# Five reciprocals of softmax sums as a power with exponent minus one on GpSimd, in a two-stage attention kernel with a token mixer

## The chip, the cores and the metric

The kernel runs on one core of a Trainium2 chip. The metric is the device time of one execution in microseconds (us). The kernel before takes 119.73 us, the median of three runs (119.31 to 119.91). The core has five engines that run at the same time, each through its own queue of instructions, in order: TensorE (PE in the profile; its weight loads are PEld), VectorE (DVE), ScalarE (ACT), GpSimd (POOL) and SyncE (SP). They wait for one another by semaphores. Loads are issued by GpSimd, stores by SyncE.

## The reference

For each of 8 batches and 8 heads there are 576 queries, keys and values of 64 numbers and 32 "packed" queries p. The first attention lets p attend to the keys; the second lets the queries attend to the result, so its softmax is only 32 wide. A token mixer with three weight matrices follows.

```python
def sm_attn(qq, kk, vv):
    s = scale * np.matmul(qq, kk.transpose(0, 1, 3, 2))
    s = s - np.max(s, axis=-1, keepdims=True)
    a = np.exp(s)
    a = a / (np.sum(a, axis=-1, keepdims=True) + 1e-09)
    return np.matmul(a, vv)
p_packed = sm_attn(p, k, v)
x = sm_attn(q, p_packed, p_packed)        # heads put side by side: [8, 576, 512]

wq, wk = x @ w_q, x @ w_k                 # 64 wide
W_tok = scale2 * einsum('bsd,btd->bst', wq, wk)
out = np.maximum(einsum('bst,btd->bsd', W_tok, x), 0.0) @ w_out
```

The change touches the division in the second attention: the sums are inverted, and the exponentials are multiplied with the inverses.

## The kernel before

All work goes batch by batch, b = 0 to 7, as a list of small operations, each a Python function named in `ops`. The string SCHEDULE (lines 10 to 59) is the program: it lists every operation once, in the order in which it is issued, for example `sm0@3g`: operation sm0 of batch 3 on GpSimd ("v" is VectorE, "s" ScalarE; a digit behind a colon is a bank of PSUM). Since every engine works its queue in order, the list sets the order on each engine, and batches overlap as the list interleaves them. Nothing is rearranged afterwards; only the waits between engines are derived from the tiles that the operations read and write. SLOTS gives the number of buffers of each tile, reused in turn.

The second softmax of a batch works on a tile of 128 partitions x 36 units x 32 scores (36 units hold the 8 heads and 9 blocks of 64 queries):

- e0, e1, e2 (L470, L482): scores on TensorE, into PSUM.
- mx0, mx1, mx2 (L498) and sb0, sb1, sb2 (L502): the maxima and the subtraction on VectorE.
- x0 (L531): the exponential on ScalarE, over 128x1152.
- sm0: the sums over 32. On VectorE one reduction (L537, batches 0, 2 and 7); on GpSimd a tree of five additions that halves the width (L540, three times L542, L543; batches 1, 3, 4, 5 and 6).
- rr0 (L547): the reciprocal of the 128x36 sums, on VectorE for all eight batches.
- ml0, ml1, ml2 (L551): exponentials times reciprocals, for the units 0 to 15, 16 to 31 and 32 to 35, into the bf16 tile a2. Each of the 24 runs on the engine that the list names; five run on VectorE (ml2@0, ml1@2, ml0@3, ml1@4, ml2@6), the other 19 on GpSimd.
- at0 (from ml0's units) and at1 (from ml1's and ml2's) (L571, L574): transposes of a2 on TensorE, evicted by ae0 and ae1. Later matmuls (g, L675 and L683) read a2 itself.

Other operations that stand near: LQ, LK and LV issue the loads of a batch's q, k and v on GpSimd (L148); rc1 (L369) is the reciprocal of the first softmax's sums, 128x2, and rm (L408) uses it on GpSimd; pp (L430) and pte evict the packed values of the first attention; wkx (L650) prepares an operand of g; w1 (L203) is a matmul on zeros that keeps TensorE warm and whose result nobody reads.

Where the five reciprocals stand in the list, with what is next to them on GpSimd's queue:

```
... sm0@1g rc1@3 rr0@1 LQ@4 ... ml1@1g ... ml2@1g ... ml0@1g
... sm0@3g ... LV@7 y@2 rr0@3 ml1@3g ml2@3g rc1@5 ... ml0@3v
... sm0@4g ... rr0@4 ... ml2@4g ml1@4v ... rm@6 ml0@4g
... sm0@5g rr0@5 ... ml2@5g ... ml0@5g ... ml1@5g
... sm0@6g rr0@6 ml2@6v ... ml1@6g ... ml0@6g
```

Of the kernel before, what the change touches and what calls it, by code (L numbers as in the profile page):

```python
# [20 lines left out]
    e2@1:1 mx2@1 kt1@3:2 w1@0f:4 LQ@3 ae0@0s ae1@0s LK@5 sb1@1 ke1@3s wk@0f:4 sb0@1 sb2@1 wz@0  # L21
    wke@0s kt0@3:5 ke0@3v LK@6 xt0@2f:6 wq@0:7 xe0@2v s0@3:0 rc1@2 rm@2 wkx@0 x0@1 nm0@3 wqe@0s
    qt1@2:5 qe1@2v xt1@2f:4 xe1@2s g@0f:3 ge@0s qt0@2:7 ex0@3 y@0:3 pv@2:5 qe0@2v pp@2 ye@0s m0@0:73
    r00@0v ex1@3 r01@0s pt@2c:5 pte@2v m1@0:01 xt1@3c:2 e0@2c:5 r11@0s e2@2:7 sm0@1g rc1@3 rr0@1
    LQ@4 xe1@3v ml1@1g mx2@2 ml2@1g r10@0s mx0@2 kt0@4:6 ke0@4v sb2@2 sb0@2 pq@2:3 ml0@1g pq@1:0
    pqe@2s pqe@1s LV@4 kt1@4:1 ke1@4s e1@2f:4 mx1@2 LQ@5 at1@1f:7 ae1@1s w1@0f:5 xt0@3c:6 xe0@3s
    s0@4:0 at0@1c:5 sb1@2 o2@0c:7 ae0@1v rm@3 wk@1f:5 nm0@4 wq@1:6 LK@7 LQ@6 wz@1 pv@3:3 wkx@1 x0@2
# [3 lines left out]
    e0@3f:0 r10@1s LV@6 ae0@2s mx0@3 e1@3f:7 mx1@3 LQ@7 rm@4 kt0@5:4 r00@1s wk@2f:6 ke0@5s sb0@3  # L31
    m2@1f:5 r2@1s o3@0f:1 oe3@0s sb1@3 wz@2 e2@3:0 kt1@5:3 mx2@3 wke@2s wq@2:7 sb2@3 kt1@6:0 x0@3
    sm0@3g wqe@2s ke1@5v kt0@6:2 s0@5:3 wkx@2 o1@0f:6 ke1@6v g@2f:7 ge@2s nm0@5 ex1@5 oe1@0v qt1@4:0
    ex0@5 qt0@4:7 qe0@4s ke0@6v o2@1f:6 qe1@4v xt1@5f:3 pv@4:0 LV@7 y@2:4 rr0@3 ml1@3g ml2@3g rc1@5
    oe2@1s xt0@5f:7 ye@2s ml0@3v at0@3f:2 pp@4 pt@4c:0 xe1@5s m1@2:45 r11@2s xe0@5v m0@2:61 r00@2s
    r10@2s r01@2s pte@4v e2@4:3 ae0@3v mx2@4 e1@4f:0 o4@1f:2 sb2@4 rm@5 mx1@4 st1@0 e0@4f:7 sb1@4
    mx0@4 oe4@1s at1@3f:6 ae1@3s o0@1f:5 oe0@1s s0@6:0 pq@4:4 pqe@4s sb0@4 x0@4 qt0@5:3 nm0@6
    qt1@5:6 ex0@6 qe1@5v o1@1c:4 oe1@1v kt0@7:5 kt1@7:6 wk@3f:4 ex1@6 rc1@6 sm0@4g ke0@7s xt1@6f:0
    qe0@5s ke1@7v xe1@6v wz@3 wke@3v wq@3:1 wqe@3s wkx@3 s0@7:5 qt0@6:0 qe0@6s qt1@6:2 nm0@7 ex0@7
    ex1@7 qe1@6v xt0@6f:4 o3@2f:1 rr0@4 g@3f:0 ge@3s o2@2f:2 oe2@2s st0@1 pv@5:5 ml2@4g ml1@4v  # L40
    xe0@6v y@3:3 ye@3s xt0@7f:7 xe0@7s at1@4f:2 pp@5 pt@5f:5 pte@5v oe3@2s xt1@7f:4 rm@6 ml0@4g
    at0@4f:0 m2@3f:6 r2@3s rc1@7 ae1@4v e0@5f:5 xe1@7s mx0@5 rm@7 ae0@4s e1@5f:3 o3@1f:1 oe3@1s
    o4@3f:7 wk@4f:2 oe4@3s e2@5:1 mx1@5 sb0@5 pq@5:0 pqe@5s sb1@5 wz@4 wke@4s pv@6:5 m0@3:07 mx2@5
    sb2@5 x0@5 m1@3:13 r10@3s wq@4:4 pp@6 r01@3s pt@6c:5 r00@3v r11@3s wqe@4s st2@3 qt0@7:6 pte@6v
    wkx@4 o0@2c:0 qe0@7v st0@0 e1@6c:7 mx1@6 g@4c:1 ge@4s e2@6:3 mx2@6 sb2@6 qt1@7:5 e0@6c:4 sb1@6
    o1@3c:1 mx0@6 pv@7:2 st1@1 st1@2 sm0@5g rr0@5 qe1@7s y@4:6 oe1@3s sb0@6 o1@2f:5 ye@4s st2@1
    m1@4:71 m0@4:46 pp@7 pq@6:3 oe1@2v pt@7c:2 oe0@2s st0@2 x0@6 ml2@5g o2@3c:0 r10@4s r01@4v ml0@5g
    at0@5c:6 pte@7v e0@7c:2 pqe@6v r11@4s ae0@5v e2@7:3 mx2@7 e1@7c:7 ml1@5g pq@7:1 at1@5c:5 r00@4s
    mx0@7 mx1@7 o0@3c:4 pqe@7s sb2@7 o3@3c:6 ae1@5s wk@5c:1 sb1@7 sb0@7 sm0@6g rr0@6 ml2@6v oe0@3s
    wq@5:5 oe3@3s wz@5 wke@5s o2@4c:7 wkx@5 oe2@3v st1@3 x0@7 sm0@7v ml1@6g o0@4c:3 rr0@7 ml0@6g  # L50
    wqe@5s ml0@7g ml2@7g oe0@4s g@5c:1 ge@5s o3@4c:0 oe2@4s at0@6c:6 oe3@4s y@5:4 ye@5s ae0@6v st0@3
    at1@6c:1 ae1@6v o1@4c:3 m2@5c:7 m0@5:40 r00@5v m1@5:15 oe1@4v st0@4 at0@7c:2 r2@5s r01@5s r11@5s
# [10 lines left out]
    wk=3, wkx=3, wqT=3, g=2, y=3, r=2, reluX=2, o_sb0=2, o_sb1=2, ox=2,  # L63
# [5 lines left out]
def kernel(  # L69
# [12 lines left out]
    nc = tc.nc  # L82
    fp32 = mybir.dt.float32
# [14 lines left out]
    P = 128  # L98
    NJ = S // 64
    NU = 36  # L100
# [6 lines left out]
    sbp = ctx.enter_context(tc.tile_pool(name="sbp", bufs=1))  # L107
# [7 lines left out]
    S_ = [{} for _ in range(B)]  # L115
# [5 lines left out]
    def tile(name, shape, dtype, b, key=None):  # L121
        key = key or name
        if key not in S_[b]:
            S_[b][key] = sbp.tile(shape, dtype, tag=f"{name}{(b // 2 if name in PAIRED else b) % SLOTS[name]}", name=name)
        return S_[b][key]
# [56 lines left out]
    nc.vector.memset(zero, 0.0)  # L182
    pT_bd = sbp.tile([P, B, 4, 2, L], bf16, name="pT_bd")
    nc.vector.memset(pT_bd, 0.0)
    mask = sbp.tile([P, 2, Dh], fp32, name="mask")
    nc.vector.memset(mask, 0.0)
    for g in range(4):
# [355 lines left out]
        nc.gpsimd.tensor_tensor(rs, t[:, :, 0:1], t[:, :, 1:2], op=ADD)  # L543

    @op
    def rr0(b):
        nc.vector.reciprocal(tile("rr", [P, NU, 1], fp32, b), S_[b]["rs"])  # L547

    def ml(i, b, on):
        r = slice(16 * i, min(16 * i + 16, NU))  # L550
# [245 lines left out]
    for item in SCHEDULE.split():  # L796
        name, rest = item.split("@")
# [35 lines left out]
```

## Time and profile before

| | |
|---|---|
| median of three runs | 119.73 us |
| the profiled execution, its time | 119.49 us |
| its span (first to last instruction) | 117.7 us |
| mean granted TensorE clock | 0.993 |
| busy, TensorE | 105.6 us |
| busy, VectorE | 91.1 us |
| busy, ScalarE | 88.0 us |
| busy, GpSimd | 60.1 us |
| HBM traffic over the span | 337 GB/s |

The times in the rows of the profile are in us from the span's start; "L551" is line 551 of the kernel. A timeline row gives the start, the duration, the engine, the line, the operation, what it writes and reads with the shapes, the number of instructions merged, and in brackets how long the engine sat idle before it and what released it. A group's row gives the busy time, the mean in nanoseconds and the idle time before its instructions. The chain of waits is followed back from the last instruction to what released each step. The ends of matmuls are modelled, and times on GpSimd are rough.

### The profile page before, as it was taken

To read this page: it belongs to the slowest core of one execution; us is meant where nothing else is said; L and a number is where in the kernel's file an instruction comes from. 1 tells how busy PE (TensorE), PEld (TensorE's weight loads), DVE (VectorE), ACT (ScalarE), POOL (GpSimd) and SP (SyncE) were. 2 spreads that over 40 slices of the span, in tenths; PEclk is the share of its full clock that TensorE was granted. 3 is DMA by queue.
4 is the path that set the end of the run, shared out by engine and by line. 5 is a ranking of instruction groups with operands and counts; after the bars stand their busy time and mean duration, and the time that the engine had idled before them with its cause. 6 is when DMAs were issued, how large, how long until landed. Compare 5 with 4: busy or idle time off the path is not lost.

```text
span 117.7 us, 4778 instructions
## 1 busy us (share of the span) xinstructions
PE 105.6 (90%) x2065; PEld 68.6 (58%) x2081; DVE 91.1 (77%) x184; ACT 88.0 (75%) x164; POOL 60.1 (51%) x88
## 2 busy tenths in 40 slices
PE   5997587887988999999999999999999999999950
PEld 1234456575855857778665875867566566545520
DVE  5326958999989989999999999698999967571420
ACT  5005574699879899899589999999898967678430
POOL 6965342278558994645981283606697780000000
PEclk9999999999999999999999999999999999999997
DMA  3999999999999999999999999999932174464793
GB/s 41 291 269 198 213 202 207 208 198 208 208 208 206 207 207 209 209 207 208 251 249 207 207 207 282 220 205 362 354 138 89 57 305 166 199 267 184 288 369 145
DMA packets 17925, 25.47 MB, mean 216 GB/s; under 512 B 2160, under 2 KB 14448, under 8 KB 17904
## 3 DMA queue, kind: packets, MB, share of 16 engines
q0 software_dynamic: 13920, 14.49, 73.2%
q1 hardware_dynamic: 3984, 10.68, 24.0%
q8 instruction: 16, 0.26, 0.8%
q14 instruction: 5, 0.04, 0.1%
HBM read 30.21 MB, written 9.44 MB: 337 GB/s over the span
## 4 chain that ended last, share of the span: by engine, by line
PE 63%; DMA 23%; DVE 7%; issue 2%; POOL 2%; ACT 1%; DVEq 0%; POOLq 0%
PE psum L755 27%; DMA k_sb<-in_k_dram 16%; PE psum L304 8%; DMA q_sb<-in_q_dram 7%; PE psum L421 3%; PE psum L714 3%; PE psum L571 3%; PE psum L660 3%; PE psum L376 3%; PE psum L628 2%; PE psum L470 2%; PE psum L345 2%; PE psum L683 1%; DVE nmax L355 1%; DVE kT L141 1%
## 5 line engine op out<-in xcount | busy, mean ns | idle before, releaser
L755 PE MATMUL psum<-w_out,r 128*64 128x512 bf16 (+1 forms) x208 | 30.9, 380 | 0.6 <-issue 0.3
L551 POOL TENSOR_TENSOR a<-e,rr 128x512 bf16<-128x512 f32 (+1 forms) x19 | 16.6, 891 | 7.2 <-ACT e L135 2.5
L755 PEld LDWEIGHTS <-r 128*64 128x64 bf16 (+1 forms) x216 | 12.3, 108 | 10.2 <-issue 1.1
L135 ACT ACTIVATE o_sb<-psum 128x512 f32<-128x512 f32 x24 | 14.5, 609 | 4.2 <-PE psum L755 4.2
L135 ACT ACTIVATE r<-psum 128x512 bf16<-128x512 f32 x24 | 13.3, 603 | 1.9 <-PE psum L714 1.9
L203 PE MATMUL psum<-zero 128*64 128x512 bf16 (+1 forms) x43 | 11.9, 487 | 2.5 <-DVE zero L182 1.2
L498 DVE TENSOR_REDUCE mx<-psum 128x16 f32<-128x512 f32 (+1 forms) x24 | 12.5, 551 | 1.8 <-PE psum L470 1.6
L359 ACT ACTIVATE e1T<-psum,nmax 128x576 bf16<-128x576 f32 x16 | 11.8, 740 | 2.8 <-DVE nmax L355 2.6
L502 DVE TENSOR_TENSOR e<-psum,mx 128x512 f32<-128x512 f32 (+1 forms) x24 | 12.4, 549 | 0.3
L540 POOL TENSOR_TENSOR rt<-e 128x576 f32<-128x576 f32 x5 | 7.1, 1422 | 10.3 <-ACT e L531 10.3
L355 DVE TENSOR_REDUCE nmax<-psum 128x2 f32<-128x1152 f32 x8 | 10.8, 1354 | 0.9 <-PE psum L345 0.8
L304 PE MATMUL psum<-ident,q_sb 128*64 128x128 bf16 x288 | 10.2, 220 | 0.4 <-DMA q_sb<-in_q_dram 0.4
L531 ACT ACTIVATE e<-e 128x1152 f32<-128x1152 f32 x8 | 9.3, 1164 | 1.0 <-DVE e L502 1.0
L135 ACT ACTIVATE kT<-psum 128x1280 bf16<-128x1280 bf16 (+3 forms) x8 | 8.0, 1013 | 2.3 <-PE psum L304 2.3
L304 PEld LDWEIGHTS <-q_sb 128*64 128x64 bf16 x288 | 8.6, 110 | 1.0 <-DMA q_sb<-in_q_dram 0.5
L304 PE MATMUL psum<-ident,k_sb 128*64 128x128 bf16 x252 | 9.0, 220 | 0.1
L141 DVE COPY o_sb<-psum 128x512 f32<-128x512 f32 x8 | 5.5, 685 | 4.0 <-PE psum L755 3.8
L542 POOL TENSOR_TENSOR rt<-rt 128x288 f32<-128x288 f32 (+2 forms) x15 | 7.9, 527 | 1.2
L148 POOL DMA_DIRECT2D v_sb<-in_v_dram x8 | 6.2, 779 | 4.3 <-DMA q_sb<-in_q_dram 2.4
L304 PEld LDWEIGHTS <-k_sb 128*64 128x64 bf16 x252 | 7.8, 110 | 0.9 <-issue 0.2
L203 PEld LDWEIGHTS <-zero 128*64 128x64 bf16 (+1 forms) x50 | 3.7, 116 | 7.9 <-issue 6.0
L135 ACT ACTIVATE qT<-psum 128x1024 bf16<-128x1024 bf16 (+1 forms) x7 | 7.5, 1092 | 0.6 <-PE psum L304 0.6
(95 smaller groups left out, 227.9 us busy)
## 6 DMA issues: line engine op xcount, KB each, us to landing
out_dram<-o_sb SPq DMA_DIRECT2D x14, 512.0 KB, 3.7
q_sb<-in_q_dram POOLq DMA_DIRECT2D x8, 576.0 KB, 17.2
v_sb<-in_v_dram POOLq DMA_DIRECT2D x8, 576.0 KB, 17.1
k_sb<-in_k_dram POOLq DMA_DIRECT2D x7, 576.0 KB, 18.4
k_f<-in_k_dram SPq DMA_DIRECT2D x2, 576.0 KB, 5.6
out_dram<-ox SPq DMA_DIRECT2D x4, 256.0 KB, 3.8
out_dram<-o_sb SPq DMA_DIRECT2D x4, 256.0 KB, 2.5
w_out<-in_moe_w_out_dram POOLq DMA_DIRECT2D x2, 256.0 KB, 14.9
```

The source lines that it names most:

```text
L135: nc.scalar.activation(dst, src, func, scale=scale)
L203: nc.tensor.matmul(bank(ks[0])[r], zero[:, r], zero, start=True, stop=True, skip_group_check=True,)
L304: nc.tensor.transpose(tp[64 * g2:64 * g2 + 64, gp, :, 64 * (j - j0):64 * (j - j0) + 64], S_[b][src][:, gp + 2 * g2, order[j]], ident,)
L355: nc.vector.tensor_reduce(tile("nmax", [P, 2], fp32, b), S_[b]["s1"], axis=AX, op=MAX, negate=True)
L359: nc.scalar.activation(tile("e1T", [P, NJ, 2, 64], bf16, b)[:, :, h2], S_[b]["s1"][:, h2].rearrange("a (j s) -> a j s", j=NJ), EXP, bias=S ...
L498: nc.vector.tensor_reduce(units(i, tile("mx", [P, NU, 1], fp32, b)), S_[b]["e", i], axis=AX, op=MAX)
L502: nc.vector.tensor_tensor(units(i, tile("e2", [P, NU, L], fp32, b)), S_[b]["e", i], m.to_broadcast((P, m.shape[1], L)), op=SUB,)
L531: nc.scalar.activation(e, e, EXP, scale=scale)
L540: nc.gpsimd.tensor_tensor(t, e[:, :, 0:16], e[:, :, 16:32], op=ADD)
L542: nc.gpsimd.tensor_tensor(t[:, :, 0:w], t[:, :, 0:w], t[:, :, w:2 * w], op=ADD)
L551: (nc.gpsimd if on == "g" else nc.vector).tensor_tensor(tile("a2", [P, NU, L], bf16, b)[:, r], S_[b]["e2"][:, r], S_[b]["rr"][:, r].to_bro ...
L755: nc.tensor.matmul(ps[r], src[:, i, r], w_out[:, i, :], start=(i == 0), stop=(i == 3),)
```

## The change

In batches 1, 3, 4, 5 and 6, those whose sums are made on GpSimd, the reciprocal becomes a two-input operation on GpSimd: the sums to the power of a tile of constants that hold minus one. In batches 0, 2 and 7 it stays on VectorE. The list's order is the same; rr0 keeps its place in it, which is now a place in GpSimd's queue. A tile of 128x36 constants is filled once at the start, on VectorE. In the changed kernel the lines behind the memset have numbers higher by 2, those behind rr0 by 7.

```diff
-    ... sm0@1g rc1@3 rr0@1
+    ... sm0@1g rc1@3 rr0@1g
-    ... pv@4:0 LV@7 y@2:4 rr0@3 ml1@3g ml2@3g rc1@5
+    ... pv@4:0 LV@7 y@2:4 rr0@3g ml1@3g ml2@3g rc1@5
-    ex1@7 qe1@6v xt0@6f:4 o3@2f:1 rr0@4 ...
+    ex1@7 qe1@6v xt0@6f:4 o3@2f:1 rr0@4g ...
-    ... sm0@5g rr0@5 qe1@7s ...
+    ... sm0@5g rr0@5g qe1@7s ...
-    ... sm0@6g rr0@6 ml2@6v oe0@3s
+    ... sm0@6g rr0@6g ml2@6v oe0@3s
...
+    minus1 = sbp.tile([P, NU, 1], fp32, name="minus1")
+    nc.vector.memset(minus1, -1.0)
...
     @op
-    def rr0(b):
-        nc.vector.reciprocal(tile("rr", [P, NU, 1], fp32, b), S_[b]["rs"])
+    def rr0(b, on="v"):
+        if on == "g":
+            nc.gpsimd.tensor_tensor(
+                tile("rr", [P, NU, 1], fp32, b), S_[b]["rs"], minus1, op=mybir.AluOpType.pow,
+            )
+        else:
+            nc.vector.reciprocal(tile("rr", [P, NU, 1], fp32, b), S_[b]["rs"])
```

More of the change, by code (lines that the diff above doesn't have):

```diff
@@ L23 @@
     qt1@2:5 qe1@2v xt1@2f:4 xe1@2s g@0f:3 ge@0s qt0@2:7 ex0@3 y@0:3 pv@2:5 qe0@2v pp@2 ye@0s m0@0:73
-    r00@0v ex1@3 r01@0s pt@2c:5 pte@2v m1@0:01 xt1@3c:2 e0@2c:5 r11@0s e2@2:7 sm0@1g rc1@3 rr0@1
+    r00@0v ex1@3 r01@0s pt@2c:5 pte@2v m1@0:01 xt1@3c:2 e0@2c:5 r11@0s e2@2:7 sm0@1g rc1@3 rr0@1g
     LQ@4 xe1@3v ml1@1g mx2@2 ml2@1g r10@0s mx0@2 kt0@4:6 ke0@4v sb2@2 sb0@2 pq@2:3 ml0@1g pq@1:0
@@ L33 @@
     sm0@3g wqe@2s ke1@5v kt0@6:2 s0@5:3 wkx@2 o1@0f:6 ke1@6v g@2f:7 ge@2s nm0@5 ex1@5 oe1@0v qt1@4:0
-    ex0@5 qt0@4:7 qe0@4s ke0@6v o2@1f:6 qe1@4v xt1@5f:3 pv@4:0 LV@7 y@2:4 rr0@3 ml1@3g ml2@3g rc1@5
+    ex0@5 qt0@4:7 qe0@4s ke0@6v o2@1f:6 qe1@4v xt1@5f:3 pv@4:0 LV@7 y@2:4 rr0@3g ml1@3g ml2@3g rc1@5
     oe2@1s xt0@5f:7 ye@2s ml0@3v at0@3f:2 pp@4 pt@4c:0 xe1@5s m1@2:45 r11@2s xe0@5v m0@2:61 r00@2s
@@ L39 @@
     qe0@5s ke1@7v xe1@6v wz@3 wke@3v wq@3:1 wqe@3s wkx@3 s0@7:5 qt0@6:0 qe0@6s qt1@6:2 nm0@7 ex0@7
-    ex1@7 qe1@6v xt0@6f:4 o3@2f:1 rr0@4 g@3f:0 ge@3s o2@2f:2 oe2@2s st0@1 pv@5:5 ml2@4g ml1@4v
+    ex1@7 qe1@6v xt0@6f:4 o3@2f:1 rr0@4g g@3f:0 ge@3s o2@2f:2 oe2@2s st0@1 pv@5:5 ml2@4g ml1@4v
     xe0@6v y@3:3 ye@3s xt0@7f:7 xe0@7s at1@4f:2 pp@5 pt@5f:5 pte@5v oe3@2s xt1@7f:4 rm@6 ml0@4g
@@ L45 @@
     wkx@4 o0@2c:0 qe0@7v st0@0 e1@6c:7 mx1@6 g@4c:1 ge@4s e2@6:3 mx2@6 sb2@6 qt1@7:5 e0@6c:4 sb1@6
-    o1@3c:1 mx0@6 pv@7:2 st1@1 st1@2 sm0@5g rr0@5 qe1@7s y@4:6 oe1@3s sb0@6 o1@2f:5 ye@4s st2@1
+    o1@3c:1 mx0@6 pv@7:2 st1@1 st1@2 sm0@5g rr0@5g qe1@7s y@4:6 oe1@3s sb0@6 o1@2f:5 ye@4s st2@1
     m1@4:71 m0@4:46 pp@7 pq@6:3 oe1@2v pt@7c:2 oe0@2s st0@2 x0@6 ml2@5g o2@3c:0 r10@4s r01@4v ml0@5g
     at0@5c:6 pte@7v e0@7c:2 pqe@6v r11@4s ae0@5v e2@7:3 mx2@7 e1@7c:7 ml1@5g pq@7:1 at1@5c:5 r00@4s
-    mx0@7 mx1@7 o0@3c:4 pqe@7s sb2@7 o3@3c:6 ae1@5s wk@5c:1 sb1@7 sb0@7 sm0@6g rr0@6 ml2@6v oe0@3s
+    mx0@7 mx1@7 o0@3c:4 pqe@7s sb2@7 o3@3c:6 ae1@5s wk@5c:1 sb1@7 sb0@7 sm0@6g rr0@6g ml2@6v oe0@3s
     wq@5:5 oe3@3s wz@5 wke@5s o2@4c:7 wkx@5 oe2@3v st1@3 x0@7 sm0@7v ml1@6g o0@4c:3 rr0@7 ml0@6g
```

## The prediction

> **What bounds the kernel now.** I read the page's busy shares first, then the chain that ended last, then the busy times of the stretch in which that chain stays on one engine, and last the rows around each of the five reciprocals.
>
> ```profile
> span 117.7 us, 4778 instructions
> PE 105.6 (90%) x2065; PEld 68.6 (58%) x2081; DVE 91.1 (77%) x184; ACT 88.0 (75%) x164; POOL 60.1 (51%) x88
> ```
> ```profile
> 38.72 0.27 DVE rr L547
> 39.00 0.35 DVE e L141
> ...
> 41.59 0.38 PE psum L203
> ...
> 60.51 0.03 issue
> 60.54 0.40 PE psum L571 x4
> ```
> ```profile
> 41.60:113.40 71.80, 71.04 (x1382) 46.26 (x1391) 59.21 (x114) 61.25 (x117) 34.30 (x48) 1.00 0.91 223
> ```
>
> The chain runs on loads first, then on VectorE pieces such as the two quoted, and from 41.59 to the last eviction at 113.40 on TensorE alone. In that stretch (the last line's columns are the busy time of TensorE, its weight loads, VectorE, ScalarE and GpSimd, each with its count, then the granted clock and DMA) TensorE is busy 71.04 of 71.80 us at full clock (1.00). So it has next to nothing left that a quicker release could remove, and a wait that the change adds in front of TensorE is not made up later: it moves the end by its own length. The only reciprocal of the sums on the chain is batch 1's, 0.27 us at 38.72.
>
> **The change: the price of one power.** Five reciprocals (batches 1, 3, 4, 5, 6) leave VectorE and five two-input operations of 128x36 enter GpSimd's queue. No row of before shows a power.
>
> ```profile
> L547 DVE RECIPROCAL rr<-rs 128x36 f32<-128x36 f32 x8 | 3.0, 371 | 0.3 <-POOL rs L543 0.2
> ...
> L369 DVE RECIPROCAL rrec<-rsum 128x2 f32<-128x2 f32 x8 | 1.2, 150 | 0.3 <-ACT e1T L359 0.3
> ```
> ```profile
> L498 DVE TENSOR_REDUCE mx<-psum 128x16 f32<-128x512 f32 x16 | 10.6, 684 | 1.6 <-PE psum L470 1.6
> ...
> L498 DVE TENSOR_REDUCE mx<-psum 128x4 f32<-128x128 f32 x8 | 2.3, 284 | 0.2 <-PE psum L482 0.2
> ...
> L551 DVE TENSOR_TENSOR a<-e,rr 128x512 bf16<-128x512 f32 x3 | 2.1, 691 | 0.1
> ```
> ```profile
> L551 POOL TENSOR_TENSOR a<-e,rr 128x512 bf16<-128x512 f32 x13 | 13.6, 1051 | 1.8 <-PE psum L699 1.1 <-DVE rr L547 0.6
> L540 POOL TENSOR_TENSOR rt<-e 128x576 f32<-128x576 f32 x5 | 7.1, 1422 | 10.3 <-ACT e L531 10.3
> ...
> L543 POOL TENSOR_TENSOR rs<-rt 128x36 f32<-128x36 f32 x5 | 1.2, 246 | 0.4
> ```
>
> ```profile
> 34.89 1.41 POOL L540 TENSOR_TENSOR rt<-e 128x576 f32<-128x576 f32 x1
> ...
> 38.19 0.25 POOL L543 TENSOR_TENSOR rs<-rt 128x36 f32<-128x36 f32 x1
> 38.67 0.80 POOL L148 DMA_DIRECT2D q_sb<-in_q_dram  x1 [0.23 <-issue]
> 39.50 1.06 POOL L551 TENSOR_TENSOR a<-e,rr 128x512 bf16<-128x512 f32 x1
> ```
>
> Low end: a power no dearer than the add of the same shape on the same engine, 0.25 us. High end: as long as the whole five-operation sum of a batch, 34.89 to 38.44 in batch 1 (last fence), about 3.6 us. Between them: GpSimd's pass costs (1422-246)/540 = 2.18 ns an element and 246-36x2.18 = 168 ns fixed. An iterated function, on the one engine that shows one, costs (371-150)/34 = 6.5 ns an element against (684-284)/384 = 1.04 ns for a simple pass, 6.2 times as much. A power is a logarithm and an exponential, so I take two such functions: 36 x 2.18 ns x 12.5 + 0.17 = 1.15 us, an estimate worked out from these rows. It is nearer to the add's row than to the five-operation row. Below, x is the price of one power.
>
> The Trainium skill, page GPSIMD Engine Reference, section 4.1 (Engine selection), speaks against the move: it puts elementwise work on VectorE, with GpSimd about two times slower on two-input operations. The same multiply here takes 1051 ns on GpSimd and 691 ns on VectorE, 1.5 times. By the page the reciprocal's 371 ns would become 0.74 us and the sum below 2.0 us; by the measured 1.5 it would become 0.56 us and the sum 1.6 us. I trust neither for a power, since both speak of adds and multiplies.
>
> **What is removed.** Batch 1's reciprocal is on the chain, but nothing is won there:
>
> ```profile
> 38.46 0.41 PE L376 MATMUL psum<-ident,e1T 128*64 128x128 bf16 x8
> ...
> 38.96 0.25 PE L482 MATMUL psum<-ppT,qT 128*64 128x64 bf16 x4
> ```
>
> The copy behind the reciprocal starts at 38.92 and reads transposes that end at 38.46+0.41 = 38.87; the reduce behind the copy starts at 39.26 and reads matmuls that end at 39.21. VectorE would wait for these instead: gain 0 to 0.05, taken as 0. The memset of the constant (128x36) is covered by VectorE's wait for the first k load, and would cost about 0.1 us without it:
>
> ```profile
> DVE k_sb L141 <- DMA k_f<-in_k_dram: 3.9, 2, 2.4
> ```
>
> **Batch 1.** The power sits between the sum and the load LQ@4, and the multiplies follow (GpSimd's rows stand above):
>
> ```profile
> 40.75 0.10 PEld L571 LDWEIGHTS <-a 128*128 128x128 bf16 x1
> ```
> ```profile
> 41.21 0.28 PE L574 MATMUL psum<-ident,a 128*128 128x128 bf16 x2
> ```
> ```profile
> q_sb<-in_q_dram POOLq DMA_DIRECT2D x8, 576.0 KB, 17.2
> ```
>
> Before, the reciprocal (ready at 39.00) was hidden under the issue of LQ@4; now the multiplies slip by the whole x, plus 0.07 for the step between two dependent operations of GpSimd, as the timeline has it between the adds of the sum. The first multiply ends at 40.56, its first weight load is at 40.75: 0.14 us of room after a release of 0.05. The transposes end at 41.49 and the warming matmul behind them starts at 41.59, held by VectorE: 0.1 more. So TensorE loses x+0.07-0.24, about x-0.15: 1.00 us. LQ@4 itself issues x later; it takes a median 17.2 us to land, which I read as a queue that is full in front of it, so that costs nothing; were the queue empty, its 1.15 us would meet transposes that are late by 1.00 anyway.
>
> **Batch 3.** Here the load LV@7 stands between the sum and the power in GpSimd's queue:
>
> ```profile
> 59.10 0.24 POOL L543 TENSOR_TENSOR rs<-rt 128x36 f32<-128x36 f32 x1
> 59.58 0.80 POOL L148 DMA_DIRECT2D v_sb<-in_v_dram  x1 [0.23 <-issue]
> ```
> ```profile
> 59.37 0.38 DVE L547 RECIPROCAL rr<-rs 128x36 f32<-128x36 f32 x1 [0.18 <-POOL rs L543]
> ...
> 59.79 0.69 DVE L551 TENSOR_TENSOR a<-e,rr 128x512 bf16<-128x512 f32 x1
> ```
>
> Today VectorE picks up the sum 0.03 us after it ends and multiplies at 59.79, ending at 60.48; the transposes of that product start at 60.54, so they have no room. After, the power starts when LV@7 has been issued, 60.38, and VectorE's multiply starts at about 60.40+x+0.05. It is late by x+0.66 even though it stayed on VectorE, and behind it wait pp@4 and two evictions on VectorE, which TensorE needs next. TensorE loses x+0.66 = 1.81 us; the largest term.
>
> **Batches 4, 5 and 6.**
>
> ```profile
> 70.18 0.25 POOL L543 TENSOR_TENSOR rs<-rt 128x36 f32<-128x36 f32 x1
> 72.53 0.84 POOL L551 TENSOR_TENSOR a<-e,rr 128x128 bf16<-128x128 f32 x1 [2.10 <-PE psum L683]
> ```
> ```profile
> 72.02 0.37 DVE L547 RECIPROCAL rr<-rs 128x36 f32<-128x36 f32 x1
> ```
> ```profile
> 83.74 0.24 POOL L543 TENSOR_TENSOR rs<-rt 128x36 f32<-128x36 f32 x1
> 84.81 2.41 POOL L551 TENSOR_TENSOR a<-e,rr 128x128 bf16<-128x128 f32 x3 [0.83 <-DVE rr L547]
> 87.19 1.43 POOL L540 TENSOR_TENSOR rt<-e 128x576 f32<-128x576 f32 x1
> ```
> ```profile
> 90.51 0.25 POOL L543 TENSOR_TENSOR rs<-rt 128x36 f32<-128x36 f32 x1
> 91.32 2.09 POOL L551 TENSOR_TENSOR a<-e,rr 128x512 bf16<-128x512 f32 x2 [0.56 <-DVE rr L547]
> ```
> ```profile
> 87.99 0.28 PEld L571 LDWEIGHTS <-a 128*64 128x64 bf16 x8
> ...
> 93.61 0.44 PEld L571 LDWEIGHTS <-a 128*64 128x64 bf16 x8
> ```
>
> In batch 4 the sum was ready at 70.43 and GpSimd idled for 2.10 us. The page names TensorE as the releaser, but the reciprocal ended at 72.39, and 0.14 us from VectorE's end to GpSimd's start is also what batches 5 and 6 show, so I read it as the releaser. Up to 2.0 us of power is free, and TensorE gains nothing, as it had other work. In batch 5 the multiplies started 0.83 us after the sum; they now start 0.10+x after it, late by x-0.73 = 0.42. Their last one ended at 87.22, and its transposes load at 87.99: covered up to x = 1.4. But the sum of batch 6 began at 87.19 right behind them, so it slips by the same 0.42, and its own power adds x-0.46 (0.56 of the wait less 0.10): the multiplies of batch 6 are late by 2x-1.19. The last ended at 93.41; their weight loads begin at 93.61, the matmuls some 0.2 later, 0.3 of room: TensorE loses 2x-1.5 = 0.80. VectorE's share of batch 6 waits for the same power, with g's operand behind it, and gives about the same.
>
> **Sum.** 1.00 + 1.81 + 0 + 0 + 0.80 = 3.61 us on the profiled execution's 119.49, 123.1. That execution lies 0.24 under the median of the runs, 119.73; on the median it is 123.3. At x = 0.25: 0.10+0.91 = 1.0, 120.7. At x = 3.6: 3.45+4.26 in batches 1 and 3, 1.6 in batch 4, 2.2 in 5 and 3.5 in 6, together 15.0, 134.8.
>
> **Rivals.**
> *VectorE was the bound (faster).* Five times 0.371 us leave it, 1.86 us; if TensorE really waits on VectorE throughout, and the power hides, the time is 117.9. For it: VectorE is at 77% overall and feeds TensorE in every batch. Against: 59.21 of 71.80 us in the long stretch, no VectorE piece on the chain there. It decides only if x is under 0.3 and batch 3's multiply finds room behind LV@7.
> *Hidden after all (no change).* TensorE catches up on both stalls, because the ends of its matmuls are modelled and it may be less full than 71.04 of 71.80; 119.7. Against: the row at 60.51 shows 0.03 us between the product's release and its use.
> *The power is done lane by lane and far beyond any row.* At x = 10 nothing is covered: 9.85+10.66+8.0+8.6+9.9 is 47 us, 167 us. For it: no row prices a power. Against: every other GpSimd operation here costs about 2 ns an element.
> *The first power alone is dear,* a one-time start on GpSimd, paid in batch 1 where there is 0.24 us of room. The first sum on GpSimd, batch 1's, shows no such thing (1.41 us against a mean of 1.422); the only idle of GpSimd there that no engine explains is the 0.23 us before a load, and so much more gives 123.5. The same page of the Trainium skill, section 2.1, gives about 6 us for the first call to freshly loaded code, which as an estimate would make it 129; no row here shows it.
>
> **Numbers.** The forecast, x between 0.25 and 3.6 with both stalls exposed: 0.76. First power dear: 0.04. Far beyond: 0.11. No change: 0.05. Faster: 0.04. The range 120.0 to 135.0 holds the first two, 0.80; its low end lies 0.7 under the sum at x = 0.25, for room in front of TensorE that I don't see. About 0.5% (0.6 us) is what this kernel can tell from no change; the hidden stalls make up the 0.05 within it, the VectorE rival the 0.04 below, and the rest, 0.91, is slower.
>
> **What would show it.** The five new rows on GpSimd give x directly. Batch 1: multiplies about x later behind LQ@4, and a TensorE weight load of L571 waiting on GpSimd. Batch 3: VectorE idle for over a microsecond before its multiply, released by GpSimd, and LV@7 between sum and power. Batch 4: multiplies earlier, TensorE unmoved. Batch 6: sum and multiplies later. I am wrong if x lies far from 1.15 us, or if TensorE shows idle time at 41 and 60 us and yet ends as before.

## The result and the profile after

The changed kernel takes 153.48 us (median of four runs, 153.09 to 153.70) against 119.82 us for the kernel before, a ratio of 1.281 with a 95% interval of 1.274 to 1.287. Slower was forecast, but with 123.3 us and a range that ended at 135.0.

The page of the profile after: span, busy shares, the granted clock in 40 slices, the chain by engine, and the group of the new operations.

```profile
span 151.7 us, 4792 instructions
PE 118.2 (78%) x2081; PEld 74.6 (49%) x2081; DVE 89.8 (59%) x180; ACT 89.0 (59%) x164; POOL 91.6 (60%) x93
...
PEclk9999999999975899998579995599975895999999
...
POOL 36%; PE 32%; DMA 18%; ACT 6%; issue 4%; DVE 2%; POOLq 0%; DVEq 0%
...
L550 POOL TENSOR_TENSOR rr<-rs,minus 128x36 f32<-128x36 f32 x5 | 30.7, 6150 | 0.3
```

One power takes 6.15 us, not 1.15. GpSimd, 2% of the chain before, is now its largest part, and the line of the granted clock (PEclk) has five dents. They go with five stalls of TensorE. Its timeline, the first matmuls behind each stall, with the idle time before them in brackets:

```profile
46.65 0.61 PE L578 MATMUL psum<-ident,a 128*128 128x128 bf16 x4 [5.21 <-POOL a L558]
74.19 0.61 PE L578 MATMUL psum<-ident,a 128*128 128x128 bf16 x4 [6.45 <-DVE a L558]
92.98 0.32 PE L706 MATMUL psum<-pp,g 64*64 64x128 bf16 x3 [3.83 <-DVE e L141]
113.27 0.64 PE L578 MATMUL psum<-ident,a 128*64 128x128 bf16 x8 [4.38 <-POOL a L558]
124.68 0.25 PE L682 MATMUL psum<-wkx,a 128*64 128x128 bf16 x2 [3.12 <-DVE wkx L657]
```

These are batches 1, 3, 4, 5 and 6, together 22.99 us. The rest of the loss shows in the busy time of the stretch from 41.6 us to the last matmul (columns as in the prediction's windows row):

```profile
41.60:147.30 105.70, 82.76 (x1398) 52.53 (x1398) 58.43 (x111) 62.83 (x117) 65.61 (x56) 0.85 0.62 152
```

The same stretch was 71.80 us long before, with 71.04 busy; it is 105.70 long, with 82.76 busy. So 22.2 us of the difference are idle time. Of the 11.7 us more of busy time, 0.6 are six transposes of batch 1, which fall into this stretch only after the change; the other 11 or so are matmuls that take longer, at a mean granted clock of 0.85. Two groups of sixteen output matmuls, one right behind batch 5's stall and one after it, show it:

```profile
115.52 3.51 PE L762 MATMUL psum<-w_out,r 128*64 128x512 bf16 x16
...
119.67 1.89 PE L762 MATMUL psum<-w_out,r 128*64 128x512 bf16 x16
```

GpSimd's timeline in batches 1 and 3: the load and the multiplies stand behind the power as forecast, and in batch 3 LV@7 stands between the sum and the power.

```profile
38.54 6.16 POOL L550 TENSOR_TENSOR rr<-rs,minus 128x36 f32<-128x36 f32 x1
44.67 0.84 POOL L148 DMA_DIRECT2D q_sb<-in_q_dram  x1
45.53 2.40 POOL L558 TENSOR_TENSOR a<-e,rr 128x512 bf16<-128x512 f32 x3
...
65.93 0.25 POOL L545 TENSOR_TENSOR rs<-rt 128x36 f32<-128x36 f32 x1
66.41 0.81 POOL L148 DMA_DIRECT2D v_sb<-in_v_dram  x1 [0.24 <-issue]
67.24 6.17 POOL L550 TENSOR_TENSOR rr<-rs,minus 128x36 f32<-128x36 f32 x1
```

Theory after this look: the waits are those of the forecast, with another price; and each long stall costs more than its length, because TensorE's clock falls. Its rivals: the price is a start-up of some kind; the loss is one of GpSimd's load as a whole, not of places; the longer matmuls are not the clock.

### The profile page after: what moved, and what is told of

Same layout as the page of the kernel before. It is cut to its first block, busy times and chain, and to the rows that moved or that the text cites. A ratio compares the mean times of both kernels' runs of the same rounds, so it can differ in the third digit from the quotient of the medians.

```text
span 151.7 us, 4792 instructions
## 1 busy us (share of the span) xinstructions
PE 118.2 (78%) x2081; PEld 74.6 (49%) x2081; DVE 89.8 (59%) x180; ACT 89.0 (59%) x164; POOL 91.6 (60%) x93
## 4 chain that ended last, share of the span: by engine, by line
POOL 36%; PE 32%; DMA 18%; ACT 6%; issue 4%; DVE 2%; POOLq 0%; DVEq 0%
POOL rr L550 20%; PE psum L762 15%; DMA k_sb<-in_k_dram 12%; DMA q_sb<-in_q_dram 6%; POOL rt L544 5%; POOL rt L542 5%; PE psum L578 3%; ACT e L533 2%; POOL a L558 2%; PE psum L721 2%; PE psum L378 2%; PE psum L306 2%; PE psum L472 1%; PE psum L635 1%; PE psum L347 1%
## 5 line engine op out<-in xcount | busy, mean ns | idle before, releaser
L762 PE MATMUL psum<-w_out,r 128*64 128x512 bf16 (+1 forms) x216 | 35.5, 417 | 0.1
L550 POOL TENSOR_TENSOR rr<-rs,minus 128x36 f32<-128x36 f32 x5 | 30.7, 6150 | 0.3
L578 PE MATMUL psum<-ident,a 128*64 128x128 bf16 (+1 forms) x92 | 8.4, 277 | 16.0 <-POOL a L558 9.6
L558 POOL TENSOR_TENSOR a<-e,rr 128x512 bf16<-128x512 f32 (+1 forms) x19 | 17.2, 923 | 5.2 <-ACT e L135 3.7
L762 PEld LDWEIGHTS <-r 128*64 128x64 bf16 (+1 forms) x216 | 13.6, 118 | 12.1 <-issue 4.4
L205 PE MATMUL psum<-zero 128*64 128x512 bf16 (+1 forms) x50 | 14.1, 470 | 1.6 <-DVE zero L182 1.2
L578 PEld LDWEIGHTS <-a 128*64 128x64 bf16 (+1 forms) x92 | 5.9, 138 | 18.7 <-POOL a L558 10.4
L500 DVE TENSOR_REDUCE mx<-psum 128x16 f32<-128x512 f32 (+1 forms) x24 | 12.5, 551 | 4.1 <-PE psum L472 2.4
L558 DVE TENSOR_TENSOR a<-e,rr 128x512 bf16<-128x512 f32 (+1 forms) x5 | 2.7, 530 | 18.1 <-POOL rr L550 18.1
L504 DVE TENSOR_TENSOR e<-psum,mx 128x512 f32<-128x512 f32 (+1 forms) x24 | 12.5, 552 | 0.3
L141 DVE COPY a2T<-psum 128x512 bf16<-128x512 bf16 (+1 forms) x9 | 4.3, 478 | 12.9 <-PE psum L578 12.2
```

Of the source, the lines that this page charges most:

```text
L205: nc.tensor.matmul(bank(ks[0])[r], zero[:, r], zero, start=True, stop=True, skip_group_check=True,)
L500: nc.vector.tensor_reduce(units(i, tile("mx", [P, NU, 1], fp32, b)), S_[b]["e", i], axis=AX, op=MAX)
L504: nc.vector.tensor_tensor(units(i, tile("e2", [P, NU, L], fp32, b)), S_[b]["e", i], m.to_broadcast((P, m.shape[1], L)), op=SUB,)
L550: nc.gpsimd.tensor_tensor(tile("rr", [P, NU, 1], fp32, b), S_[b]["rs"], minus1, op=mybir.AluOpType.pow,)
L558: (nc.gpsimd if on == "g" else nc.vector).tensor_tensor(tile("a2", [P, NU, L], bf16, b)[:, r], S_[b]["e2"][:, r], S_[b]["rr"][:, r].to_bro ...
L578: nc.tensor.transpose(tp[r, h2, P * c:P * c + P], a2(b, 2 * i + c, h2)[:, r], ident)
```

## The experiments

**What one power costs.** The kernel before, with operations at the end of GpSimd's queue whose results nobody reads.

```diff
+        nc.gpsimd.tensor_tensor(spare[:, 0:36], rs, minus1[:, 0:36], op=ADD)
+        nc.gpsimd.tensor_tensor(spare[:, 0:36], rs, minus1[:, 0:36], op=POW)
+        nc.gpsimd.tensor_tensor(spare[:, 0:9], e[:, 0:9], minus1[:, 0:9], op=POW)
+        nc.gpsimd.tensor_tensor(spare[:, 0:18], e[:, 0:18], minus1[:, 0:18], op=POW)
+        nc.gpsimd.tensor_tensor(spare[:, 0:72], e[:, 0:72], minus1[:, 0:72], op=POW)
+        nc.gpsimd.tensor_tensor(spare[0:64, 0:36], rs[0:64], minus1[0:64, 0:36], op=POW)
+        nc.gpsimd.tensor_tensor(spare[:, 0:36], minus1[:, 0:36], rs, op=MULT)
```

> The kernel before, with seven operations more at the end of GpSimd's queue, where it has nothing left to do: an add, a power and a multiply of 128x36, powers of 128x9, 128x18 and 128x72, and one of 64x36. Theory (the power works element by element behind a small fixed cost): 0.25 us for the add and the multiply, 6.15 for the power of 36, about 1.7 for 9, 3.2 for 18 and 12.1 for 72, and 6.15 for 64 partitions, since the partitions go side by side. Rival (a fixed cost, such as code that is called or fetched at each power): about 6 us for all widths. Second rival (the first power alone is dear, and each of the five of the change was a first one again because other operations came between): the first of the row 6.15 and the ones behind it far less.

GpSimd's timeline:

```profile
97.20 0.26 POOL L194 TENSOR_TENSOR rt<-rs,minus 128x36 f32<-128x36 f32 x1
97.54 6.16 POOL L195 TENSOR_TENSOR rt<-rs,minus 128x36 f32<-128x36 f32 x1
103.78 1.80 POOL L196 TENSOR_TENSOR rt<-e,minus 128x9 f32<-128x9 f32 x1
105.66 3.22 POOL L197 TENSOR_TENSOR rt<-e,minus 128x18 f32<-128x18 f32 x1
108.95 11.88 POOL L198 TENSOR_TENSOR rt<-e,minus 128x72 f32<-128x72 f32 x1
120.91 6.11 POOL L199 TENSOR_TENSOR rt<-rs,minus 64x36 f32<-64x36 f32 x1
127.10 0.26 POOL L200 TENSOR_TENSOR rt<-minus,rs 128x36 f32<-128x36 f32 x1
```

From 9 to 72 elements a power grows by (11.88-1.80)/63 = 160 ns an element, with 0.36 us fixed. An element of a simple pass was 2.18 ns, so a power is some 73 passes. Half the partitions cost the same. Both rivals fall: the cost isn't the same for all widths, and the powers that follow one another directly lie on the same line as the first.

**The places, at a small price.** The add of the same shape in the power's place, in the same queue.

```diff
-                tile("rr", [P, NU, 1], fp32, b), S_[b]["rs"], minus1, op=mybir.AluOpType.pow,
+                tile("rr", [P, NU, 1], fp32, b), S_[b]["rs"], minus1, op=ADD,
```

> The changed kernel with an add in the place of the power, so the factors are the sums less one and the output is another. Everything else, the queue and its waits, stays. Theory (the step that failed is the power's price alone, and the waits are as forecast): x = 0.25 gives 0.10 in batch 1 and 0.91 in batch 3, 1.0 us more than the kernel before, 120.8 us, a ratio of 1.008, and TensorE waits about 0.9 us for VectorE's multiply in batch 3 at about 60 us. Rival (with a cheap operation the move hides or gains, and the queue place of LV@7 is harmless): 119.0 to 119.8, a ratio of 0.993 to 1.000.

120.06 us, a ratio of 1.0034 (1.0015 to 1.0054): a loss of 0.41 us where 1.0 was expected, and not the gain or nothing of the rival. VectorE's and TensorE's timelines in batch 3:

```profile
60.39 0.69 DVE L558 TENSOR_TENSOR a<-e,rr 128x512 bf16<-128x512 f32 x1 [1.05 <-POOL rr L550]
```
```profile
61.14 0.40 PE L578 MATMUL psum<-ident,a 128*128 128x128 bf16 x4 [0.55 <-DVE a L558]
```

The wait is where the forecast put it, 0.55 us instead of 0.91. The part that is missing lies ahead of it: the sum of batch 3 starts 0.07 us after its exponential has ended, where it was 0.48 before. The exponential on ScalarE and the start of the sum on GpSimd, first before, then with the add:

```profile
54.13 1.16 ACT L531 ACTIVATE e<-e 128x1152 f32<-128x1152 f32 x1
```
```profile
55.77 1.43 POOL L540 TENSOR_TENSOR rt<-e 128x576 f32<-128x576 f32 x1 [1.26 <-ACT e L531]
```
```profile
54.22 1.17 ACT L533 ACTIVATE e<-e 128x1152 f32<-128x1152 f32 x1
```
```profile
55.46 1.42 POOL L542 TENSOR_TENSOR rt<-e 128x576 f32<-128x576 f32 x1 [0.81 <-ACT e L533]
```

The gap is the long one in all runs in which batch 1's reciprocal is VectorE's, and the short one in those with batch 1 on GpSimd. The trace of the kernel before has a separate semaphore instruction of 17 ns in front of the sums of batches 3 to 6, that of the add version has none. That it waits for GpSimd's own earlier result, which the operation on GpSimd has already waited for, is read from the kernel. That this wait is the cause is argued and not shown: batch 4's sum has one too, and starts 0.15 us after its exponential.

**The same, ahead of LV@7.**

```diff
-    ... pv@4:0 LV@7 y@2:4 rr0@3g ml1@3g ...
+    ... pv@4:0 y@2:4 rr0@3g LV@7 ml1@3g ...
```

> The kernel with the add in the place of the power, and the add of batch 3 ahead of LV@7; the output is another, as there. Theory (what the add version lost, 0.41 us, is the 0.81 us issue of LV@7 in VectorE's wait, less a sum of batch 3 that starts 0.4 us sooner): the loss goes, 119.3 to 119.7, a ratio of 0.997 to 1.001. Rival (the loss is elsewhere): 120.0, a ratio of 1.003.

119.44 us, a ratio of 1.0001 (0.9971 to 1.003). The interval overlaps a little with that of the version before, so the times alone don't tell the two apart; TensorE's timeline does. Its transposes of that product start without a wait:

```profile
60.31 0.39 PE L578 MATMUL psum<-ident,a 128*128 128x128 bf16 x4
```

So it was the issue of the load. An operation at the price of an add, placed well, gave no change within 0.3% and no gain, although 1.86 us had left VectorE.

**The order alone, with the real power.** The same edit of the list in the changed kernel.

> The changed kernel with the power of batch 3 ahead of the load LV@7 in GpSimd's queue instead of behind it. Theory (the issue of the load is part of what VectorE's multiply of batch 3 waits for): 0.8 to 1.0 us less, 152.5, because the idle time of TensorE there falls from 6.45 to about 5.5. Rival (the load is hidden beside something else, or the later load costs as much): no change, 153.5.

153.04 us, a ratio of 1.2806 (1.276 to 1.285) to the kernel before, the changed kernel's own ratio. Batch 3's stall shrinks as expected, but batch 1's is longer and the clock a little lower:

```profile
46.70 0.61 PE L578 MATMUL psum<-ident,a 128*128 128x128 bf16 x4 [5.55 <-POOL a L558]
73.54 0.61 PE L578 MATMUL psum<-ident,a 128*128 128x128 bf16 x4 [5.45 <-DVE a L558]
```

Inconclusive for the end: the stall lost 1.0 us, of which 0.4 at most arrived in the median. The traced execution, 153.76 us, is the slowest of its four; the others took 152.88 to 153.06, and how much of that is the order isn't separated from how one run differs from the next (here 0.34 us in batch 1, and the granted clock from 0.899 to 0.893).

**The clock.** The changed kernel, with matmuls on zeros in front of each wait, so that TensorE is busy while it waits (w24 is 24 of 128x512).

```diff
-    ... at1@1f:7 ... at0@3f:2 ... y@3:3 ... at0@5c:6 ... g@5c:1 ...
+    ... w24@1f:7 at1@1f:7 ... w28@1f:2 at0@3f:2 ... w18@1f:3 y@3:3
+    ... w20@1f:6 at0@5c:6 ... w14@1f:1 g@5c:1 ...
```

> The changed kernel with matmuls on zeros in front of the five waits of TensorE, 24, 28, 18, 20 and 14 of 128x512, about as many as fit at 0.216 us each; nobody reads their results. Theory (of the 33.7 us lost about 23 are idle time of TensorE and about 11 a lower clock around the stalls): the granted clock goes from 0.90 to about 0.98 and the time falls by 8 to 11 us, to 143 to 146; what is left is 23 us of waits. Rival (the longer matmuls after a stall are not the clock, or the zeros don't hold it): no change or up to 2 us more.

150.81 us at a clock of 0.989. The direction is the theory's, the size isn't, and TensorE's timeline says why: the zeros in front of batch 5's g had been given bank 1, which is itself released late, and so ran after the wait instead of during it.

```profile
119.08 0.59 PE L205 MATMUL psum<-zero 128*128 128x512 bf16 x1 [5.63 <-DVE wkx L657]
```

A second version has them write bank 4:

> As the kernel with the zeros, but the 14 in front of batch 5's g write bank 4 instead of bank 1. In the first one they waited for bank 1 until 119.0 us, as the real matmul does, and then ran 3.7 us in its way, so that it measured the clock and a loss of its own. Theory (the clock was worth about 7 us of the 33.8): 4 to 4.5 us less than the first, 146.0 to 147.0, with the clock at 0.98 or more. Rival (the zeros in the way cost nothing, the clock is worth 2.7 us): 150.8.

```profile
PEclk9999999999999999999999999999999987999999
...
L205 PE MATMUL psum<-zero 128*128 128x512 bf16 (+1 forms) x154 | 37.1, 406 | 1.6 <-DVE zero L182 1.2 <-DVE kT L141 0.4
L762 PE MATMUL psum<-w_out,r 128*64 128x512 bf16 (+1 forms) x216 | 32.6, 389 | 0.0
```

147.25 us, a ratio of 1.232 (1.228 to 1.237), clock 0.988; the time is a little over the 146.0 to 147.0 expected. Of the five dents one shallow one is left, and an output matmul (L762) takes 389 ns in the mean, against 417 in the changed kernel and 380 before. So at least 6.2 of the 33.7 us were the clock, by work that computes nothing. The dent that is left stands at batch 5's g, where the zeros end before the wait does. TensorE's timeline there, and the windows row of the work behind it, at a granted clock of 0.50:

```profile
118.93 0.32 PE L682 MATMUL psum<-wkx,a 128*64 128x128 bf16 x2 [2.50 <-DVE wkx L657]
```
```profile
118.93:122.00 3.07, 3.07 (x38) 2.05 (x37) 2.27 (x4) 1.28 (x3) 2.21 (x3) 0.50 0.43 169
```

**One batch at a time.** The power in one batch only; the others as before. The edit of the list for batch 1; the other four are made the same way:

```diff
-    ... rr0@1g ... rr0@3g ... rr0@4g ... rr0@5g ... rr0@6g ...
+    ... rr0@1g ... rr0@3 ... rr0@4 ... rr0@5 ... rr0@6 ...
```

> Only batch 1 has the power on GpSimd, the other seven reciprocals are VectorE's. Theory (the forecast's terms at the measured price of 6.15 us, plus a slow clock behind each stall): TensorE idle for 5.2 to 6.0 us at about 41 us and 1.5 to 2 us more by the clock behind it, 126.3 to 127.6 us. Rival (the loss of the five is one of GpSimd's total load and not of places): a fifth of the 33.8 us lost, 126.4 here and the same in each single batch.

> Only batch 3 has the power on GpSimd, behind the issue of LV@7. Theory: x+0.66 = 6.8 us of idle TensorE at about 60 us less up to 0.4, since the sum comes earlier than forecast, and 1.5 to 2 us by the clock, 127.5 to 128.4. Rival (a fifth of the loss each): 126.4.

> Only batch 4 has the power on GpSimd; before, GpSimd sat idle for 2.1 us between this sum and its multiplies. Theory: x-2.0 = 4.15 us or a little less of idle TensorE at about 74 us, and 1 to 2 us by the clock, 124.4 to 125.8, the cheapest of the batches 1, 3 and 4. Rival (a fifth of the loss each): 126.4.

> Only batch 5 has the power on GpSimd. Theory: x-1.4 = 4.75 us of idle TensorE or a little less at about 87 us, the sum and the multiplies of batch 6 late behind it but covered by that stall, and 1.5 to 2 us by the clock, 125.7 to 126.8. The five single losses would then add up to 35 to 36 us, over the 33.8 of all five together, because the stall of batch 5 and its slow clock cover part of batch 6's. Rival (batch 6 adds a second stall of its own behind it): 128 or more.

> Only batch 6 has the power on GpSimd. Theory (its own price counts once, x-0.46 less 0.3 of room, and the 3.1 us of idle time seen with all five are what is left of it behind batch 5's stall and slow clock): 5.4 us of idle TensorE at about 93 us and 1 to 2 us by the clock, 125.8 to 127.0. Rival (the 3.1 us seen are its own price, the rest was room): 123.5 to 124.5.

TensorE's timeline, the stall of each of the five kernels (batch 1, 3, 4, 5, 6), one fence each:

```profile
46.67 0.61 PE L578 MATMUL psum<-ident,a 128*128 128x128 bf16 x4 [5.17 <-POOL a L558]
```
```profile
67.31 0.61 PE L578 MATMUL psum<-ident,a 128*128 128x128 bf16 x4 [6.85 <-DVE a L558]
```
```profile
78.03 0.25 PE L706 MATMUL psum<-pp,g 64*64 64x128 bf16 x3 [3.91 <-DVE e L141]
```
```profile
91.85 0.64 PE L578 MATMUL psum<-ident,a 128*64 128x128 bf16 x8 [4.46 <-POOL a L558]
```
```profile
97.98 0.32 PE L682 MATMUL psum<-wkx,a 128*64 128x128 bf16 x2 [4.90 <-DVE wkx L657]
```

| power only in | time, us | lost, by the ratio | lost in the traced execution | its stall | beyond the stall | work behind it at clock 0.50, us | forecast's term at 6.15 us |
|---|---|---|---|---|---|---|---|
| batch 1 | 126.52 | 7.0 | 6.88 | 5.17 | 1.71 | 3.8 | 6.0 |
| batch 3 | 128.24 | 9.2 | 8.50 | 6.85 | 1.65 | 4.2 | 6.8 |
| batch 4 | 125.70 | 6.2 | 5.63 | 3.91 | 1.72 | 3.4 | 4.15 |
| batch 5 | 125.46 | 5.9 | 6.03 | 4.46 | 1.57 | 3.0 | 4.75 |
| batch 6 | 126.87 | 7.3 | 7.23 | 4.90 | 2.33 | 4.3 | 5.4 (alone) |

The loss differs from place to place, so the rival of a fifth each (126.4 everywhere) falls. Stalls come out within 0.9 us of the terms, always below but for batch 3. Four of the times lie in the bands expected, batch 5's 0.24 us under its own. The ratios of batches 3 and 4 are uncertain by about 1 us (intervals 1.066 to 1.088 and 1.043 to 1.060), so the loss beyond the stall is taken from the execution whose trace shows the stall: 1.6 to 2.3 us. (The traced executions took 126.52, 128.14, 125.27, 125.64 and 126.87 us, against medians before of 119.64 and, for batch 5, 119.61.) Half of the time worked at clock 0.50 is 1.5 to 2.2 us, within 0.5 us of that loss each time. What the extra loss is stands in TensorE's timeline behind the stall of the kernel with batch 1 alone, and at the same place of the kernel before (there with the lines L345 and L755):

```profile
48.38 1.17 PE L347 MATMUL psum<-kT,pT_bd 128*64 128x512 bf16 x8
...
49.77 1.41 PE L762 MATMUL psum<-w_out,r 128*64 128x512 bf16 x8
51.11 0.47 PE L635 MATMUL psum<-pqk,a2T 128*128 128x64 bf16 x10
```
```profile
42.20 0.66 PE L345 MATMUL psum<-kT,pT_bd 128*64 128x512 bf16 x8
...
42.91 1.03 PE L755 MATMUL psum<-w_out,r 128*64 128x512 bf16 x8
43.88 0.47 PE L628 MATMUL psum<-pqk,a2T 128*128 128x64 bf16 x10
```

From 46.67 to some point in the output matmuls at 50 us everything takes about twice as long; from 51.1 on the durations are the old ones. The windows row of that time in the kernel with batch 1 alone:

```profile
46.67:50.50 3.83, 3.83 (x37) 2.49 (x39) 0.48 (x2) 2.56 (x3) 3.82 (x6) 0.50 1.21 208
```

A bit under 4 us at half speed costs a bit under 2 us. The Trainium skill, page TensorE: Matmul & The Clock Gate, Part 1, says that the array runs at half rate after an idle window of about 3.4 us and until a busy window of that length has passed. The five stalls of these kernels are all longer than that and agree, as do the 3.0 to 4.3 us of slow work behind them. But two shorter stalls were followed by a clock of 0.50 as well, the 3.12 us of batch 6 in the changed kernel and the 2.50 us of the second version with zeros; there the measurement decides. The 0.55 us of the add version left the clock at 0.996; nothing between was isolated. The clock can also fall late: behind the 3.12 us it was 1.00 until about 125.6 us, 0.9 us after the stall had ended, and then 0.50 until 129.0.

The five single losses sum to 35.6 by the ratios and to 34.3 by the traced executions, against 33.7 for all five at once, which is too close to tell. What overlaps shows in the stalls: batch 6's is 4.90 alone and 3.12 together. In the changed kernel, TensorE works at half speed behind batch 5's stall, as its windows row shows:

```profile
113.27:118.60 5.33, 5.33 (x76) 3.58 (x78) 3.31 (x7) 1.79 (x3) 4.94 (x7) 0.50 0.01 2
```

These 5.3 us delay it by some 2.7 us before it comes to batch 6's wait, whose end is set by GpSimd and VectorE. So slow work behind one stall covered part of the next, which agrees with the expectation for batch 6.

**Occupied queue or awaited result.** Five powers into a tile that nobody reads, and VectorE's reciprocals as before.

```diff
-                tile("rr", [P, NU, 1], fp32, b), S_[b]["rs"], minus1, op=mybir.AluOpType.pow,
+                spare, S_[b]["rs"], minus1, op=mybir.AluOpType.pow,
             )
-        else:
+        if True:
             nc.vector.reciprocal(tile("rr", [P, NU, 1], fp32, b), S_[b]["rs"])
```

> The changed kernel with the five powers written to a tile that nobody reads; the factors come from VectorE's reciprocals as before. GpSimd is occupied as in the changed kernel, but VectorE waits for no power. Theory (in batches 1, 4 and 5 it is the occupied queue that makes the loss, in 3 and 6 VectorE's wait in part): 1.5 to 3 us less than the changed kernel, 150.5 to 152; batch 3's stall falls from 6.45 to about 4.8. Rival (the wait for the result makes the loss, and an occupied GpSimd alone is harmless): 120 to 125.

TensorE's stalls in batches 3 and 4 of this kernel:

```profile
73.96 0.61 PE L579 MATMUL psum<-ident,a 128*128 128x128 bf16 x4 [4.17 <-POOL a L559]
89.19 0.29 PE L582 MATMUL psum<-ident,a 128*128 128x128 bf16 x2 [2.46 <-POOL a L559]
90.77 0.61 PE L579 MATMUL psum<-ident,a 128*128 128x128 bf16 x4 [0.95 <-POOL a L559]
```

148.94 us, ratio 1.246 (1.241 to 1.250), clock 0.924. Nearly nine tenths of the loss stay though nobody needs the powers: it is the occupied queue, with the twelve multiplies of these batches behind the powers. The stall of batch 3 shrinks by 2.3 us, more than expected, and now waits for GpSimd; that of batch 4 comes in two pieces, together 0.4 us shorter than the 3.83. The clock dips less, and the time is 1.6 us under the expected band.

## Why the prediction was wrong

- *What bounds the kernel.* Right in kind: each of the five waits put in front of TensorE alone came out at the end. But "by its own length" failed: a stall of 3.9 to 6.9 us cost 1.6 to 2.3 us more, by the clock. The forecast read the granted clock of 1.00 and did not ask what a stall does to it.
- *The price of one power.* This step failed: 1.15 us was taken, 6.15 measured. The step took a power for two functions, each as much dearer than a pass as VectorE's reciprocal is, 12.5 passes on GpSimd; it is 73 passes, 160 ns an element. VectorE's reciprocal gave no price for it. The high end, 3.6 us, was the longest stretch at hand and no bound; the rival "far beyond any row", priced at 10 us and given 0.11, was right in kind, and 6.15 lies between the two. The argument against it, that other operations cost about 2 ns an element, was of adds and multiplies.
- *The rule on the choice of engine.* The factor of two from the Trainium skill, page GPSIMD Engine Reference, section 4.1 (Engine selection), and the measured 1.5 of the multiply were rightly not trusted for a power: it takes 16.6 times the reciprocal's 0.371 us.
- *The removed reciprocals bring nothing.* Right within 0.3%: a ratio of 1.0001 with the operations at an add's price and the load behind.
- *The places.* Right in kind in all five batches. Batch 3 was the largest term, with LV@7 ahead of the power and VectorE stuck behind it. Batch 4's 2.0 us of free room held (a stall of 3.91 alone for a power of 6.15), though TensorE's wait there came through VectorE's multiply and an eviction behind it, which the forecast didn't name. Batch 5's came out at 4.46 for 4.75. At the measured price the recorded terms give 6.00+6.81+4.15+4.75+6.05 = 27.8 us, 147.6 on the median. The stalls of the changed kernel sum to 22.99, and most of the difference is batch 6, 3.12 for 6.05: slow work behind batch 5 had already delayed TensorE. With the clock mostly held by zeros, the wait there is 118.93-113.24 = 5.69 us from the start of the zeros at 113.24 us, and the loss 147.25-119.61 = 27.6. The closeness to 27.8 owes something to luck, as other stalls are some tenths under their terms and about 1.5 us of slow clock are still in it.
- *What was missed beside the price:* at least 6 us of slow clock, which the sum put at nothing, and a sum in batch 3 that starts 0.4 us sooner, which took 0.4 of the 0.9 us of that wait at a small price.
- *The first power alone is dear.* No: the five take 6139 to 6165 ns, the first among them.
- *What would show it.* x from the rows, the stall of L578 at batch 1, VectorE idle in batch 3 all came as named. In batch 4 the multiplies came later and not earlier, as follows from x over 2.0.

## What to carry to other kernels

An operation that no row shows has no price by analogy with another engine: measure it first, at the idle end of a queue, at two widths, before forecasting any wait. In a kernel that runs on one engine without gaps, where a new operation stands in its queue matters beside what it costs: the load ahead of the power, and the multiplies behind it, made the loss even when nobody needed the result. And a TensorE stall of some 4 us or more, here already of 2.5 us, should be charged about 2 us more for the clock, unless the next wait covers it.

## What the runs showed of the hardware

- A power of two f32 tensors on GpSimd: 0.36 us and 160 ns for each element of a partition, nearly the same for 64 and 128 partitions (6.11 and 6.16 us at 36 elements); an add or a multiply of 128x36: 0.26 us.
- Behind an idle time of 2.5 to 6.9 us TensorE's granted clock was 0.50, and its matmuls took about twice as long, for 3.0 to 5.3 us of work; it fell during the stall, or up to 0.9 us behind it. Matmuls on zeros that nobody reads, issued during the wait, kept the clock at 0.988 in the mean.
- The start of an operation on GpSimd behind ScalarE's result took 0.48 us in one place and 0.07 in the same place with one wait fewer; the cause stays open.
